# The first two slots of a seven-product MLP in plain form, x parts made in place, no splits on GpSimd

## The chip, the cores and the metric

One core of a Trainium2 chip runs the whole program. The metric is the device time in microseconds (us) of one execution, as the median of several. The engines are TensorE (PE, with its weight loads as PEld), VectorE (DVE), ScalarE (ACT), GpSimd (POOL) and SyncE (SP), which here only issues DMAs; GpSimd issues DMAs too.

## The reference

Linear attention, then two MLPs, all in float32:

```
kv  = einsum("bhsd,bhse->bhde", k, v)            # 4 batches, 8 heads, 576 tokens, 64 wide
o   = einsum("bhsd,bhde->bhse", q, kv)
x   = o / sqrt(mean(o*o) + 1e-6) * g_norm        # as 2304 tokens x 512
y   = softplus(x @ w1) @ w2                      # 512 -> 2048 -> 512
out = leaky_relu(y @ w3, 0.01) @ w4              # 512 -> 2048 -> 512
```

## The kernel before, in words

**Attention** runs over 16 units (a batch and a pair of heads). T transposes q and k and forms k^T v, O multiplies, `normal` normalizes, and X (four units behind) transposes the result into the tile `xy`, which holds x^T for all tokens. Units up to 9 use the PSUM banks 0 to 3, later ones 0 and 1, with further banks for O and X.

**Split numbers.** A float32 operand of an MLP is kept as a high part, rounded by a ScalarE copy (`fp32r`), and a low part, what is left, by a VectorE or GpSimd subtraction (`split_part`, lines 711 and 706; `split_pair`, 655 and 659; `split_w2`, 612 and 618). A product is three matmuls: high by high, high by low, low by high. The weights come as 64-bit floats and are decoded into float32 first (`decode_w`: one ScalarE and three VectorE operations, lines 578 to 596, with two raw buffers).

**Seven products.** The first layer of an MLP works on blocks of 2 x 2: two halves of the 512 inputs, two token halves of 384, two feature blocks of 128. A slot `s` multiplies one pair of token halves (`t = s // 2`, 768 tokens; three pairs, NTP = 3) by 256 features (`u = s % 2`). It uses the form with seven block products instead of eight, of six matmuls each (`product`, line 802). For this, sums of blocks of x are made by `x_part`: parts 0, 3 and 5 are plain blocks, and parts 1, 2, 4 and 6 are differences made one from the other through two tiles `xt` (line 740), and each is split. The sums of the weights' blocks come from `split_pair` (line 638). `after` puts the seven results together: copies (line 825) and additions (line 832) into `cA` and `cB`, the activation (839 or 845), and the split of the result (853, 858). `quarter` is the second layer (lines 900 and 916, 48 matmuls in a slot from the third on), and adds into `xy`.

**Where the parts of x lie.** The tile `xe` (in `ra`) holds seven parts for the pair in work. For the first pair they are made in place during attention, and stored to a DRAM scratch `xscr`. For the next pairs, at first sight, `x_part` makes the difference parts during the even slot in two stages in `rc` and stores them to `xscr` (line 758); in the odd slot, when a product has used its old part, `x_load` loads the new one on GpSimd's queue (line 784), and splits the plain blocks from `xy` or from a load on SP's queue (line 775). The eight groups of 512 features (four for each MLP) go over the same three pairs, with x parts from `xscr` after the first group of an MLP.

**The order of the work** is not the program's. Every operation is handed to a planner (`Plan`) with a cost for each engine that may do it, what it reads and writes, and a due time worked back from the matmuls. The planner plays the run through, picks for every engine what is due first, and so fixes the order of each engine's queue and the engine for what several could do (`either`: VectorE or GpSimd). An engine's queue is in order. The planner holds a load issued on GpSimd's queue for done after 1.0 us, one on SP's queue after its transfer and fixed times.

```
wst, xe: ra;  raw weights, xt, cA[0], cB: mf;  stages: rc;  cA[1], second raw weight pair: lf
slot s:  seven times  product(s, i); after(s, i); [x_part or x_load for t + 1]; a seventh of the quarters
```

Of the kernel before, what the change touches and what calls it, by code (L numbers as in the profile page):

```python
# [19 lines left out]
class Plan:  # L20
# [8 lines left out]
    IDLE = 40.0  # L29
    DMA_ISSUE, DMA_START, DMA_DONE = 0.57, 1.1, 1.0  # L30

    def __init__(self):
# [30 lines left out]
    def span(self, o):  # L63
        if "S" in o["cost"]:
            return self.DMA_ISSUE + self.DMA_START + o["cost"]["S"] + self.DMA_DONE
        return min(o["cost"].values())

    def run(self):
        for o in reversed(self.ops):
            for s in o["succ"]:  # L70
                o["due"] = min(o["due"], s["due"] - self.LAT - self.span(o))
        free = {e: 0.0 for e in ("PE", "A", "D", "P", "S", "N")}
        dma = 0.0
# [15 lines left out]
        while True:  # L89
            best = None  # L90
            for e, c in cand.items():
                if not c:
                    continue
                t = max(free[e], min(o["at"][e] for o in c))
# [15 lines left out]
            o["eng"], o["start"] = e, t  # L110
            if e == "S":
                free[e] = t + self.DMA_ISSUE
# [16 lines left out]
def linear_attention_two_mlps(  # L129
# [32 lines left out]
    nc = tc.nc  # L162
# [57 lines left out]

    SIZE = {"ra": 70, "mf": 24, "rb": 54, "rc": 12, "lf": 7}
    bufs = {}
# [41 lines left out]
    sqr = const.tile([P, DM], I32, name="sqr")  # L264
    raw = [Reg("mf", at * KI, [DM, 2], I32) for at in (0, 4)]

    SRAW = (("mf", 8), ("lf", 0))
    sraw = [Reg(n, at * KI, [4, 256]) for n, at in SRAW]
# [63 lines left out]
    def copy_to(out, in_, n, reads, writes):  # L332
# [222 lines left out]
    def decode_w(F, which, a_reg):  # L555
        ph, f = F // NF, F % NF
        src = ((w1, w2), (w3, w4))[ph][which]
        ri = chunk_no[0] % 2
        chunk_no[0] += 1
        r_, t_ = raw[ri].ap, sqr  # L560
        low, high = r_[:, :, 0], r_[:, :, 1]

        def f_l(e):
            if which == 0:
                nc.sync.dma_start(
# [3 lines left out]
            else:  # L569
# [3 lines left out]

        rk, tk, ak = raw[ri].keys(), [("sqr",)], a_reg.keys()
        op({"S": 1.46}, f_l, (), rk)
        op(
            {"A": t_a(DM)},
            lambda e: nc.scalar.activation(  # L578
                a_reg.ap.bitcast(F32), high.bitcast(F32), AF.Copy, scale=2.0 ** -112
            ), rk, ak,  # L580
# [24 lines left out]

    def split_w2(F, i, beside=False):
        for m in range(2):
# [8 lines left out]
            op(  # L616
                either(DM, beside),
                lambda e, d_=d_, w_=w_: ENG[e].tensor_tensor(
# [13 lines left out]

    def split_pair(i, u, beside=False):
        r, w_ = sraw[i], wst[u]

        def combine(j, a, b, sign):
            def fn(e):
                ENG[e].tensor_tensor(r[:, j, :], r[:, a, :], r[:, b, :], sign)

            op(either(256, beside), fn, part(r, a) + part(r, b), part(r, j))  # L640

        def parts(j, at, n):
# [18 lines left out]
            op({"A": t_a(m)}, hi, sk, hk)  # L661
            op(either(m, beside), lo, sk + hk, lk)


        parts(1, 0, 3)
        combine(1, 0, 1, ALU.add)
# [33 lines left out]

    def split_part(e_, src, sk, beside=False):
        n = 2 * BN
# [16 lines left out]
    def x_part(tp, i, stages=()):  # L719


        def B(j, k_):
            return x_block(tp, j, k_)

        if i in PLAIN:
            src, sk = B(*PLAIN[i])
            if not stages:
                split_part(xe[i], src, sk, True)
            op(
                {"S": 1.2}, lambda e: nc.sync.dma_start(out=whole(tp, i), in_=src()),  # L730
                sk, [("xs", tp, i)],
            )
            return
# [4 lines left out]
        def minus(t, a, b):  # L738
            def fn(e):
                ENG[e].tensor_tensor(xt[t].ap, a[0](), b[0](), ALU.subtract)  # L740

            op(either(2 * BN, not stages), fn, a[1] + b[1], xt[t].keys())
            return T_(t)
# [8 lines left out]
        if stages:  # L752
            e_ = stages[stage_no[0] % len(stages)]
            stage_no[0] += 1
        split_part(e_, src, sk, not stages)
        op(
# [5 lines left out]
    def flat(e_):  # L762
        return Reg(e_.name, e_.at, [4 * BN])

    xt_no = [0]

    def x_load(tp, i, at_hand):
# [3 lines left out]
        if i in PLAIN:  # L771
# [16 lines left out]
    def u_bank(s, which):  # L788

        return (s % 2, 2, 3)[which] if s else (2, 3, 3)[which]  # L790

    def product(s, i):
# [19 lines left out]
        op({"PE": 6 * t_mm[BN]}, fn, wk + e_.keys(), [("ps", bank)])  # L812

    def after(s, i):

# [19 lines left out]

        def act(dst, src, n, reads, writes):
            if s < 2 * NG * NTP:
                op(
                    {"A": t_a(n)}, lambda e: nc.scalar.activation(dst(), src(), AF.Softplus),  # L839
                    reads + [("set", 0)], writes + [("set", 1)],  # L840
                )
                return
            op(
                {"A": t_a(n)},
                lambda e: nc.scalar.activation(dst(), src(), AF.Prelu, alpha=0.01),  # L845
                reads + [("set", 1)], writes,
            )

        def parts(c, g):
            n = 2 * BN  # L850
            gk = g.keys(0, 4 * n)
            op(
                {"A": t_a(n)}, lambda e: nc.scalar.activation(g[:, 0, :, :], c.ap, AF.Copy),  # L853
                c.keys(), gk,
            )
            op(
                {"D": t_d(n)},
                lambda e: nc.vector.tensor_tensor(  # L858
                    g[:, 1, :, :], c.ap, g[:, 0, :, :].bitcast(F32), ALU.subtract
                ),  # L860
                c.keys() + gk, g.keys(4 * n),
            )

        if i == 0:
# [7 lines left out]
        elif i == 4:  # L872
            plus(cB, 0, U, bu)
            act(lambda: cB.ap, lambda: cB.ap, 2 * BN, cB.keys(), cB.keys())
            parts(cB, gB[s % 2])
        elif i == 5:
            plus(cA_, 1, W, bw)
            act(lambda: cA_[:, 1, :], lambda: cA_[:, 1, :], BN, ck(cA_, 1), ck(cA_, 1))
        else:
            act(lambda: cA_[:, 0, :], lambda: U, BN, bu, ck(cA_, 0))  # L880
            parts(cA_, gA[s % 3])
# [66 lines left out]
    def norm_done(e):  # L948
# [3 lines left out]
        )  # L952
        buf(p, "rc", F32R)
        buf(p, "lf", F32)
# [16 lines left out]
    for i in range(NU + XL):  # L971
# [4 lines left out]
        if i >= XL:  # L976
# [17 lines left out]
       + [(t + "r", i) for t in "qkv" for i in range(2)])  # L994
    split_w2(0, 0, True)
    op({"N": 0.0}, norm_done, (), granules("rc", "lf") + [("sql", 0)]
# [3 lines left out]
    decode_pair(2, 1, 1)  # L1000
    split_w2(2, 1, True)

# [4 lines left out]
    for s in range(2 * NT2 + 2):  # L1007
# [74 lines left out]
```

## Time and profile before

| | us |
|---|---|
| median of 3 runs (lowest, highest) | 858.88 (854.82, 860.17) |
| the profiled execution | 858.63 |
| its span, first to last instruction | 856.9 |

Busy in the span: TensorE 830.3 us, its weight loads 772.8, VectorE 572.2, ScalarE 449.5, GpSimd 97.6. DMA moved 172.73 MB. In the rows below an arrow `out<-in` names tiles, `L802` a line of the kernel, and `[2.44 <-DMA ra<-xscr]` says that the engine sat idle 2.44 us before and what it waited for. An instruction's length in a row overlaps a little with the next one's of the same engine.

### The profile page before, as it was taken

To read this page: it belongs to the slowest core of one execution; us is meant where nothing else is said; L and a number is where in the kernel's file an instruction comes from. 1 tells how busy PE (TensorE), PEld (TensorE's weight loads), DVE (VectorE), ACT (ScalarE), POOL (GpSimd) and SP (SyncE) were. 2 spreads that over 40 slices of the span, in tenths; PEclk is the share of its full clock that TensorE was granted. 3 is DMA by queue.
4 is the path that set the end of the run, shared out by engine and by line. 5 is a ranking of instruction groups with operands and counts; after the bars stand their busy time and mean duration, and the time that the engine had idled before them with its cause. 6 is when DMAs were issued, how large, how long until landed. Compare 5 with 4: busy or idle time off the path is not lost.

```text
span 856.9 us, 11971 instructions
## 1 busy us (share of the span) xinstructions
PE 830.3 (97%) x4512; PEld 772.8 (90%) x4512; DVE 572.2 (67%) x911; ACT 449.5 (52%) x730; POOL 97.6 (11%) x152
## 2 busy tenths in 40 slices
PE   7998879999999999999999999999999999999997
PEld 5877769999999999999999998898988889898986
DVE  2779958786558673877778875766568855854332
ACT  1567847666445553645456665755455544553340
POOL 1476210000000000000000000000000000100000
PEclk9999999999999999999999999999999999999999
DMA  9984679667527646547757867645635852643613
GB/s 280 319 260 173 202 283 342 228 209 229 188 88 235 202 142 225 170 153 229 244 198 236 310 242 269 223 165 190 227 95 181 275 172 82 203 147 93 203 49 98
DMA packets 80024, 172.73 MB, mean 202 GB/s; under 512 B 11616, under 2 KB 54112, under 8 KB 79968
## 3 DMA queue, kind: packets, MB, share of 16 engines
q1 hardware_dynamic: 66720, 99.63, 35.0%
q0 software_dynamic: 13248, 72.36, 25.4%
q8 instruction: 35, 0.57, 0.3%
q14 instruction: 21, 0.17, 0.1%
HBM read 141.30 MB, written 30.67 MB: 201 GB/s over the span
## 4 chain that ended last, share of the span: by engine, by line
PE 88%; DMA 5%; DVE 4%; ACT 2%; issue 1%; POOL 0%; SPq 0%; POOLq 0%; DVEq 0%
PE ps L802 38%; PE ps L900 22%; PE ps L916 22%; PE ps L436 2%; DMA ra<-xscr 1%; DMA mf<-in_moe_w_in_dram 1%; PE ps L405 1%; DMA xscr<-rc 1%; PE ps L397 1%; PE ps L528 1%; DMA qa<-in_q_dram 1%; PE ps L442 1%; PE ps L408 1%; DVE xn L506 0%; DVE ra L659 0%
## 5 line engine op out<-in xcount | busy, mean ns | idle before, releaser
L802 PE MATMUL ps<-ra 128*128 128x384 f32 x2016 | 406.0, 336 | 10.0 <-DMA ra<-xscr 7.7
L802 PEld LDWEIGHTS ps<-ra 128*128 128x128 f32 x2016 | 357.4, 188 | 27.0 <-issue 6.5
L900 PE MATMUL ps<-rb 128*128 128x384 f32 x1152 | 227.1, 335 | 0.0
L916 PE MATMUL ps<-rb 128*128 128x512 f32 x864 | 225.0, 394 | 0.4 <-ACT xy L678 0.4
L900 PEld LDWEIGHTS ps<-rb 128*128 128x128 f32 x1152 | 202.6, 188 | 0.0
L916 PEld LDWEIGHTS ps<-rb 128*128 128x128 f32 x864 | 159.7, 188 | 24.7 <-ACT xy L678 1.1
L832 DVE TENSOR_TENSOR mf<-ps,mf 128x384 f32<-128x384 f32 x120 | 66.7, 557 | 156.5 <-PE ps L802 124.5
L784 POOL DMA_DIRECT2D ra<-xscr x92 | 49.2, 535 | 653.4 <-PE ps L802 605.5
L825 ACT ACTIVATE mf<-ps 128x384 f32<-128x384 f32 x120 | 58.7, 492 | 99.2 <-PE ps L802 98.5
L683 DVE TENSOR_TENSOR xy<-ps,xy 128x384 f32<-128x384 f32 (+1 forms) x126 | 77.4, 614 | 30.1 <-PE ps L916 20.8
L858 DVE TENSOR_TENSOR rb<-mf,rb 128x768 fp32r<-128x768 f32 x72 | 68.4, 951 | 1.9 <-ACT rb L853 1.8
L711 ACT ACTIVATE ra<-mf 128x768 fp32r<-128x768 f32 x58 | 48.7, 841 | 29.8 <-PE ps L802 28.6
L853 ACT ACTIVATE rb<-mf 128x768 fp32r<-128x768 f32 x72 | 61.0, 847 | 2.1
L706 DVE TENSOR_TENSOR ra<-mf,ra 128x768 fp32r<-128x768 f32 x55 | 53.5, 972 | 12.3 <-ACT ra L711 12.0
L845 ACT ACTIVATE mf<-mf 128x768 f32<-128x768 f32 (+1 forms) x36 | 26.6, 739 | 60.1 <-DVE mf L832 60.1
L839 ACT ACTIVATE mf<-mf 128x768 f32<-128x768 f32 (+1 forms) x36 | 26.5, 735 | 45.5 <-DVE mf L832 45.5
L590 DVE SCALAR_TENSOR_TENSOR sqr<-mf,sqr 128x512 int32<-128x512 int32 x64 | 46.9, 733 | 1.2
L578 ACT ACTIVATE mf<-mf 128x512 f32<-128x512 f32 x34 | 22.6, 666 | 27.4 <-DMA mf<-in_moe_w_in_dram 19.8
L678 ACT ACTIVATE xy<-ps 128x384 f32<-128x384 f32 (+1 forms) x33 | 17.4, 531 | 18.0 <-PE ps L900 14.7
L858 DVE TENSOR_TENSOR rb<-lf,rb 128x768 fp32r<-128x768 f32 x24 | 22.9, 954 | 3.7 <-ACT rb L853 3.7
L832 DVE TENSOR_TENSOR lf<-ps,lf 128x384 f32<-128x384 f32 x24 | 13.4, 558 | 16.9 <-PE ps L802 16.8
L596 DVE SCALAR_TENSOR_TENSOR mf<-mf,sqr 128x512 int32<-128x512 int32 x34 | 23.7, 698 | 0.4
(97 smaller groups left out, 646.5 us busy)
## 6 DMA issues: line engine op xcount, KB each, us to landing
ra<-xscr POOLq DMA_DIRECT2D x92, 768.0 KB, 6.0
mf<-xscr SPq DMA_DIRECT2D x54, 384.0 KB, 5.5
mf<-in_moe_w_in_dram SPq DMA_DIRECT2D x32, 512.0 KB, 4.4
mf<-in_moe_w_out_dram SPq DMA_DIRECT2D x32, 512.0 KB, 4.0
xscr<-rc SPq DMA_DIRECT2D x20, 768.0 KB, 4.0
xscr<-xy SPq DMA_DIRECT2D x18, 384.0 KB, 4.8
qa<-in_q_dram SPq DMA_DIRECT2D x16, 256.0 KB, 5.2
ka<-in_k_dram SPq DMA_DIRECT2D x16, 256.0 KB, 5.1
```

The lines of the kernel that those rows point to most:

```text
L590: lambda e: nc.vector.scalar_tensor_tensor(t_, low, 29, t_, ALU.logical_shift_right, ALU.bitwise_or), rk + tk, tk,
L683: {"D": t_d(n)}, lambda e: nc.vector.tensor_tensor(dst, src, dst, ALU.add),
L706: ENG[e].tensor_tensor(e_[:, 1, :, :], src(), e_[:, 0, :, :].bitcast(F32), ALU.subtract)
L711: {"A": t_a(n)}, lambda e: nc.scalar.activation(e_[:, 0, :, :], src(), AF.Copy),
L784: lambda e: nc.gpsimd.dma_start(out=flat(xe[i]).ap, in_=xscr[7 * tp + i]),
L802: nc.tensor.matmul(o, w_[:, a, c:c + P], e_[:, b, kk, :], start=(not on and kk == 0 and n == 0), stop=(kk == 1 and n == 2), skip_group_che ...
L825: {"A": t_a(BN)}, lambda e: nc.scalar.activation(c[:, m, :], src, AF.Copy),
L832: lambda e: nc.vector.tensor_tensor(c[:, m, :], src, c[:, m, :], ALU.add),
L853: {"A": t_a(n)}, lambda e: nc.scalar.activation(g[:, 0, :, :], c.ap, AF.Copy),
L858: lambda e: nc.vector.tensor_tensor(g[:, 1, :, :], c.ap, g[:, 0, :, :].bitcast(F32), ALU.subtract),
L900: nc.tensor.matmul(y[:, :BN], w_[m][:, a, js], G_[:, b, m, :], start=(u == 0 and m == 0 and i == 0), stop=(u == 1 and m == 1 and i == 2),)
L916: nc.tensor.matmul(y, G_[:, a, m, js], w_[m][:, b, :], start=(u == 0 and m == 0 and i == 0), stop=(u == 1 and m == 1 and i == 2),)
```

## The change

- Slots 0 and 1 (t = 0) use a plain form with eight block products (`plain`). They read four split blocks of x, not sums, and write banks 2 and 3 only. `first_blocks` splits these four and stores them unsplit. One more block of W is split for each slot (`wx`, in the place of part 3 of x).
- For t = 1 and 2 `x_part` makes the parts in place in `xe`, in the odd slot before. The parts of the first pair are made in slot 5 from blocks loaded back in slot 4 (`blocks_back`, into `rc`) and stored for later groups. The second MLP's first group is staged as before.
- `either` goes: all splits, sums and differences are VectorE's. GpSimd keeps copies of q and k, some small operations of `normal`, and its DMA loads.
- The planner counts a load on GpSimd's queue (`"G"`) with issue, start, transfer and end, as one on SP's queue.
- `lf` grows to 8 KB and `mf` shrinks to 23: `cA[1]` moves to `mf` and the second raw buffer to `lf`, which exists only after attention; the first six weight chunks use one raw buffer.

```diff
-        if "S" in o["cost"]:
-            return self.DMA_ISSUE + self.DMA_START + o["cost"]["S"] + self.DMA_DONE
+        if self.DMA_BY.keys() & o["cost"].keys():
+            return self.DMA_ISSUE + self.DMA_START + sum(o["cost"].values()) + self.DMA_DONE
...
-    raw = [Reg("mf", at * KI, [DM, 2], I32) for at in (0, 4)]
+    raw = [Reg(n, at * KI, [DM, 2], I32) for n, at in (("mf", 0), ("lf", 4))]
...
+    wx = [Reg("ra", at * KI, [2, 256]) for at in (18, 20)]
...
-        ri = chunk_no[0] % 2
+        ri = chunk_no[0] % 2 if chunk_no[0] >= 6 else 0
...
-        op(either(n, beside), lo, sk + hk, lk)
+        op({"D": t_d(n)}, lo, sk + hk, lk)
...
-            {"P": 1.0},
+            {"G": 2.25},
             lambda e: nc.gpsimd.dma_start(out=flat(xe[i]).ap, in_=xscr[7 * tp + i]),
...
-        return (s % 2, 2, 3)[which] if s else (2, 3, 3)[which]
+        return (s % 2, 2, 3)[which]
...
+    FIRST = {(0, 0): 0, (1, 0): 1, (0, 1): 5, (1, 1): 6}
+
+    def first_blocks():
+        for (j, k_), at in FIRST.items():
+            src, sk = x_block(0, j, k_)
+            split_part(xe[at], src, sk)
+            x_store(0, {(0, 0): 0, (1, 1): 3, (1, 0): 5, (0, 1): 7 * NTP}[j, k_], src, sk)
...
+    def plain(s, k_):
+        c, g_ = (cB, gB[s % 2]) if k_ else (cA[s % 2], gA[s % 3])
+        w_ = wst[s % 2]
+        for m in range(2):
+            o = ps[2 + m][:, :BN]
+            for j in range(2):
+
+                e_, W_, part_ = xe[FIRST[j, k_]], *((wx[s], 0) if m + j == 0 else (w_, 2 * m + j - 1))
...
+                op({"PE": 6 * t_mm[BN]}, fn, wk + e_.keys(), [("ps", 2 + m)])
+            from_psum(c[:, m, :], o, BN, 2 + m, c.keys(4 * BN * m, 4 * BN * (m + 1)))
+        act(s, lambda: c.ap, lambda: c.ap, 2 * BN, c.keys(), c.keys())
+        parts(c, g_)
...
             if i - XL == 2 * NPAIR - 1:
-                for part_ in range(7):
-                    x_part(0, part_)
+                first_blocks()
...
         for i in range(7):
+            if t == 0 and i in (0, 3):
+                plain(s, i // 3)
             if t < NT2:
-                product(s, i)
-                after(s, i)
-                if t + 1 < NT2 and u == 0 and t + 1 in fresh:
+                if t > 0:
+                    product(s, i)
+                    after(s, i)
+                if s == 2 * NTP - 2 and i == 0:
+                    blocks_back()
+
+
+                if t + 1 in fresh and t + 1 > NTP and u == 0:
                     x_part((t + 1) % NTP, i, xstage)
-                if t + 1 < NT2 and u == 1:
+                elif t + 1 < NTP and u == 1:
+                    x_part((t + 1) % NTP, i)
+                elif t + 1 == NTP and u == 1:
+                    x_part(0, i, B=back)
+                elif t + 1 < NT2 and u == 1:
                     x_load((t + 1) % NTP, i, t + 1 in fresh)
```

## Rows read from the trace of the kernel before

**Rows 1.** totals of the page: busy time, share of the span, instructions of each engine.

```profile
PE 830.3 (97%) x4512; PEld 772.8 (90%) x4512; DVE 572.2 (67%) x911; ACT 449.5 (52%) x730; POOL 97.6 (11%) x152
```

**Rows 2.** stretches: length, busy PE, PEld, DVE, ACT, POOL (instructions); PEclk, DMA share, GB/s.

```profile
40.00:94.00 54.00, 49.20 (x338) 40.48 (x336) 48.15 (x93) 39.11 (x82) 34.73 (x37) 1.00 0.66 224
94.00:110.00 16.00, 11.98 (x65) 11.02 (x64) 14.91 (x20) 14.70 (x23) 4.76 (x4) 0.98 0.65 221
110.00:120.00 10.00, 7.71 (x39) 7.23 (x38) 4.99 (x7) 2.63 (x5) 0.64 (x2) 0.86 1.05 391
120.00:160.00 40.00, 36.64 (x208) 35.74 (x207) 29.42 (x45) 24.96 (x44) 2.64 (x5) 1.00 0.76 271
160.00:174.00 14.00, 14.00 (x83) 14.00 (x82) 11.28 (x19) 10.31 (x18) 1.58 (x3) 1.00 0.69 220
174.00:200.00 26.00, 26.00 (x152) 26.00 (x151) 17.34 (x27) 15.11 (x26) 1.58 (x3) 1.00 0.57 194
```

**Rows 3.** TensorE's waits from 40 to 94 us: total us, times, longest.

```profile
PE ps L397 <- ACT qt L353: 2.6, 4, 0.8
PE ps L436 <- DVE xn L506: 1.1, 2, 0.9
```

**Rows 4.** TensorE's waits from 94 to 160 us.

```profile
PE ps L802 <- DMA ra<-xscr: 7.7, 4, 2.4
PE ps L802 <- ACT lf L825: 1.4, 1, 1.4
```

**Rows 5.** chain that ended last, 90 to 160 us: start, length, what.

```profile
106.29 9.87 DMA xscr<-rc
...
128.37 2.08 PE ps L802 x12
```

**Rows 6.** TensorE in order of time: start, length, line, count, idle before.

```profile
109.31 2.13 PE L802 MATMUL ps<-ra 128*128 128x384 f32 x6 [2.44 <-DMA ra<-xscr]
...
114.69 1.28 PE L802 MATMUL ps<-ra 128*128 128x384 f32 x6 [2.29 <-DMA ra<-xscr]
```

**Rows 7.** lines 706, 740, 638, 618, 659: length, VectorE busy, GpSimd busy, then as above.

```profile
30.00:124.00 94.00, 8.45 (x8) 12.36 (x6) 0.98 0.74 248
30.00:124.00 94.00, 4.42 (x4) 8.71 (x4) 0.98 0.74 248
30.00:124.00 94.00, 2.54 (x3) 3.67 (x5) 0.98 0.74 248
30.00:124.00 94.00, 0.69 (x1) 4.84 (x3) 0.98 0.74 248
30.00:124.00 94.00, 5.01 (x3) 1.81 (x1) 0.98 0.74 248
```

**Rows 8.** VectorE's groups from 180 to 400 us: busy us, mean ns of one.

```profile
L706 DVE TENSOR_TENSOR ra<-mf,ra 128x768 fp32r<-128x768 f32 x21 | 20.1, 956 | 5.7 <-ACT ra L711 5.7
...
L832 DVE TENSOR_TENSOR mf<-ps,mf 128x384 f32<-128x384 f32 x35 | 19.5, 558 | 48.9 <-PE ps L802 48.9
L590 DVE SCALAR_TENSOR_TENSOR sqr<-mf,sqr 128x512 int32<-128x512 int32 x20 | 13.8, 690 | 0.4
...
L618 DVE TENSOR_TENSOR rb<-lf,rb 128x512 fp32r<-128x512 f32 x6 | 4.1, 684 | 0.0
```

**Rows 9.** VectorE in order of time, 47 to 54 us.

```profile
47.72 0.41 DVE L638 TENSOR_TENSOR mf<-mf 128x256 f32<-128x256 f32 x1
...
53.51 1.21 DVE L659 TENSOR_TENSOR ra<-mf,ra 128x1024 fp32r<-128x1024 f32 x1
```

**Rows 10.** GpSimd and VectorE in order of time, 75 to 77 us.

```profile
75.50 2.43 POOL L740 TENSOR_TENSOR mf<-xy,mf 128x768 f32<-128x768 f32 x1
...
76.16 2.85 DVE L659 TENSOR_TENSOR ra<-mf,ra 128x1024 fp32r<-128x1024 f32 x1
```

**Rows 11.** VectorE's groups from 60 to 100 us.

```profile
L590 DVE SCALAR_TENSOR_TENSOR sqr<-mf,sqr 128x512 int32<-128x512 int32 x3 | 3.7, 1219 | 0.0
...
L638 DVE TENSOR_TENSOR mf<-mf 128x256 f32<-128x256 f32 x2 | 2.1, 1065 | 0.0
```

More of the change, by code (lines that the diff above doesn't have):

```diff
@@ L30 @@
     DMA_ISSUE, DMA_START, DMA_DONE = 0.57, 1.1, 1.0
+    DMA_BY = {"S": "S", "G": "P"}
     def __init__(self):
@@ L71, in run @@
                 o["due"] = min(o["due"], s["due"] - self.LAT - self.span(o))
-        free = {e: 0.0 for e in ("PE", "A", "D", "P", "S", "N")}
+        free = {e: 0.0 for e in ("PE", "A", "D", "P", "S", "G", "N")}
         dma = 0.0
@@ L93, in run @@
                     continue
-                t = max(free[e], min(o["at"][e] for o in c))
+                t = max(free[self.DMA_BY.get(e, e)], min(o["at"][e] for o in c))
                 o = min(
@@ L110, in run @@
             o["eng"], o["start"] = e, t
-            if e == "S":
-                free[e] = t + self.DMA_ISSUE
+            if e in self.DMA_BY:
+                free[self.DMA_BY[e]] = t + self.DMA_ISSUE
                 dma = max(dma, t + self.DMA_ISSUE + self.DMA_START) + o["cost"][e]
@@ L616, in split_w2 @@
             op(
-                either(DM, beside),
+                {"D": t_d(DM)},
                 lambda e, d_=d_, w_=w_: ENG[e].tensor_tensor(
@@ L631, in part, with split_pair @@
         return r.keys(1024 * j, 1024 * (j + n))
-    def split_pair(i, u, beside=False):
+    def split_pair(i, u, first=False):
         r, w_ = sraw[i], wst[u]
@@ L638, in fn @@
                 ENG[e].tensor_tensor(r[:, j, :], r[:, a, :], r[:, b, :], sign)
-            op(either(256, beside), fn, part(r, a) + part(r, b), part(r, j))
+            op({"D": t_d(256)}, fn, part(r, a) + part(r, b), part(r, j))
         def parts(j, at, n):
@@ L661, in parts @@
             op({"A": t_a(m)}, hi, sk, hk)
-            op(either(m, beside), lo, sk + hk, lk)
+            op({"D": t_d(m)}, lo, sk + hk, lk)
+        if first:
+            x_, hk = wx[u], wx[u].keys()
+            op({"A": t_a(256)}, lambda e: nc.scalar.activation(x_[:, 0, :], r[:, 0, :], AF.Copy),
+               part(r, 0), hk)
+            op(
+                {"D": t_d(256)},
+                lambda e: nc.vector.tensor_tensor(
+                    x_[:, 1, :], r[:, 0, :], x_[:, 0, :].bitcast(F32), ALU.subtract
+                ), part(r, 0) + hk, hk,
+            )
         parts(1, 0, 3)
@@ L713, in split_part, with x_store, x_part @@
         )
-        op(either(n, beside), lo, sk + hk, lk)
+        op({"D": t_d(n)}, lo, sk + hk, lk)
     def whole(tp, i):
         return xscr[7 * tp + i][:, :2 * BN].rearrange("p (a n) -> p a n", a=2)
-    def x_part(tp, i, stages=()):
-        def B(j, k_):
-            return x_block(tp, j, k_)
+    def x_store(tp, i, src, sk):
+        op(
+            {"S": 1.2}, lambda e: nc.sync.dma_start(out=whole(tp, i), in_=src()),
+            sk, [("xs", tp, i)],
+        )
+    def x_part(tp, i, stages=(), B=None):
+        stored = B is not None
+        B = B or (lambda j, k_: x_block(tp, j, k_))
         if i in PLAIN:
@@ L727, in x_part @@
             if not stages:
[L728 to L732, printed above, removed]
+                split_part(xe[i], src, sk)
+            if not stored:
+                x_store(tp, i, src, sk)
             return
@@ L740, in fn @@
                 ENG[e].tensor_tensor(xt[t].ap, a[0](), b[0](), ALU.subtract)
-            op(either(2 * BN, not stages), fn, a[1] + b[1], xt[t].keys())
+            op({"D": t_d(2 * BN)}, fn, a[1] + b[1], xt[t].keys())
             return T_(t)
@@ L754, in x_part @@
             stage_no[0] += 1
-        split_part(e_, src, sk, not stages)
+        split_part(e_, src, sk)
         op(
@@ L812, in product, with act @@
         op({"PE": 6 * t_mm[BN]}, fn, wk + e_.keys(), [("ps", bank)])
+    def act(s, dst, src, n, reads, writes):
+        if s < 2 * NG * NTP:
+            op(
+                {"A": t_a(n)}, lambda e: nc.scalar.activation(dst(), src(), AF.Softplus),
+                reads + [("set", 0)], writes + [("set", 1)],
+            )
+            return
+        op(
+            {"A": t_a(n)},
+            lambda e: nc.scalar.activation(dst(), src(), AF.Prelu, alpha=0.01),
+            reads + [("set", 1)], writes,
+        )
@@ new lines, in parts @@
+    def parts(c, g):
+        n = 2 * BN
+        gk = g.keys(0, 4 * n)
+        op(
+            {"A": t_a(n)}, lambda e: nc.scalar.activation(g[:, 0, :, :], c.ap, AF.Copy),
+            c.keys(), gk,
+        )
+        op(
+            {"D": t_d(n)},
+            lambda e: nc.vector.tensor_tensor(
+                g[:, 1, :, :], c.ap, g[:, 0, :, :].bitcast(F32), ALU.subtract
+            ),
+            c.keys() + gk, g.keys(4 * n),
+        )
+    FIRST = {(0, 0): 0, (1, 0): 1, (0, 1): 5, (1, 1): 6}
@@ new lines, in first_blocks, with back, blocks_back @@
+    def first_blocks():
[3 more added lines that the diff above has]
+            x_store(0, {(0, 0): 0, (1, 1): 3, (1, 0): 5, (0, 1): 7 * NTP}[j, k_], src, sk)
+    def back(j, k_):
+        x_ = xb[j, k_]
+        return (lambda: x_.ap), x_.keys()
+    def blocks_back():
+        for (j, k_), x_ in xb.items():
+            i = {(0, 0): 0, (1, 1): 3, (1, 0): 5, (0, 1): 7 * NTP}[j, k_]
+            op(
+                {"S": 1.2}, lambda e, x_=x_, i=i: nc.sync.dma_start(out=x_.ap, in_=whole(0, i)),
+                [("xs", 0, i)], x_.keys(),
+            )
@@ new lines, in plain, with fn @@
+    def plain(s, k_):
[5 more added lines that the diff above has]
+                e_, W_, part_ = xe[FIRST[j, k_]], *((wx[s], 0) if m + j == 0 else (w_, 2 * m + j - 1))
+                def fn(e, j=j, o=o, e_=e_, W_=W_, part_=part_):
+                    for kk in range(2):
+                        at = part_ * 256 + kk * P
+                        for n, (a, b) in enumerate(((0, 0), (0, 1), (1, 0))):
+                            nc.tensor.matmul(
+                                o, W_[:, a, at:at + P], e_[:, b, kk, :],
+                                start=(j == 0 and kk == 0 and n == 0),
+                                stop=(j == 1 and kk == 1 and n == 2),
+                            )
+                wk = W_.keys() if W_ is wx[s] else [
+                    k for a in range(2)
+                    for k in w_.keys(7168 * a + 1024 * part_, 7168 * a + 1024 * (part_ + 1))
+                ]
+                op({"PE": 6 * t_mm[BN]}, fn, wk + e_.keys(), [("ps", 2 + m)])
+            from_psum(c[:, m, :], o, BN, 2 + m, c.keys(4 * BN * m, 4 * BN * (m + 1)))
+        act(s, lambda: c.ap, lambda: c.ap, 2 * BN, c.keys(), c.keys())
+        parts(c, g_)
@@ L834, in plus @@
             )
[L836 to L862, printed above, removed]
         if i == 0:
@@ L952, in norm_done @@
         )
-        buf(p, "rc", F32R)
+        buf(p, "rc", F32)
         buf(p, "lf", F32)
@@ L1000, in linear_attention_two_mlps @@
     decode_pair(2, 1, 1)
-    split_w2(2, 1, True)
+    split_w2(2, 1)
     NT2 = 2 * NG * NTP
```

41 lines of the change are left out of this document (20 added, 21 removed).

## The prediction

> **What bounds the kernel now.** I read the totals first: TensorE is busy for 97% of the span and no other engine is near it [rows 1], so a gain has to come out of the few stretches in which TensorE waits, and every added matmul has to be paid. The table of stretches says where these are [rows 2]: 4.8 us of 54.0 idle between 40 and 94 us (the end of attention), 4.0 of 16 from 94 to 110, 2.3 of 10 from 110 to 120, 3.4 of 40 from 120 to 160, nothing from 160 to 200. After 160 us TensorE simply works through its matmuls; only the start can be shortened. Then the list of waits, for the two halves of the start: up to 94 us TensorE waits for ScalarE's copies of q^T (2.6 us) and for VectorE's normalized x [rows 3]; after 94 us 7.7 us stand at four waits for the load of x parts from the DRAM scratch, and 1.4 us at a copy of ScalarE behind the change of its function table [rows 4]. The chain tells why the loads are late: a staged part waits 9.9 us for its store to DRAM, and its load comes on top [rows 5]. The chip's clock also fell: the granted clock is 0.86 in the stretch with the gaps, and six products that take 1.28 us took 2.13 [rows 2, 6].
>
> **The change, part by part.** The sum is made against the profiled execution's own 858.63 us (span 856.9, 1.7 around it); the median of the runs, 858.88, is 0.25 above it, which I neglect.
>
> *No staging of x for t = 1, 2, 3.* Twelve 768 KB loads on GpSimd's queue go (four per t; 92 become 80), with their store-to-load round trips. The four waits went to these loads: **-7.7 us** [rows 4]. Bounds: 0, if TensorE then waits for the same part out of VectorE, to -7.7. I take all of it and put the new wait into a term of its own. The clock's dip goes with the gaps: 2.13 - 1.28 = **-0.9** [rows 6] (bounds 0 and -1.5; the dip covers more than the one group).
>
> *Plain form in slots 0 and 1.* 48 matmuls in place of 42, twice: 12 more. Twelve take 2.08 us in the dense stretch [rows 5]: **+2.1**, not hidden, for TensorE is the bound.
>
> *Earlier work for the gaps of attention.* Slot 0 needed differences of x made one behind the other on GpSimd; now it needs four split blocks. Slot 1 had to wait for bank 1, which attention uses to the end; plain slots use banks 2 and 3 alone, free once attention's unit 9 is through. Up to 72 matmuls (slot 0 and half of slot 1: three output buffers) can stand in the gaps up to 94 us, where 42 stood. That changes no sum of work, only fills the 4.8 us [rows 2]: bounds 0 and -4.8. The waits there are short ones behind ScalarE and VectorE [rows 3], and queues are in order, so not all are filled: three quarters, **-3.6**. The wait of 1.4 us behind the table load [rows 4] loses its place: in slot 1 TensorE writes its last two banks without the output buffer being free, and slot 2 begins in bank 0. Bounds 0 and -1.4; I take **-1.4**.
>
> *GpSimd's splits go to VectorE.* Between 30 and 124 us GpSimd did 19 of these operations: 6 splits of x, 4 differences, 5 combinations of W, 3 splits of W2, 1 of W [rows 7]. VectorE gets: four splits of first blocks where it had one of that pair, +3 x 0.956; combinations +5 x 0.41; W2 +3 x 0.684; W +0.96; two new splits of 256 columns +2 x 0.41. That is 8.9 us [rows 8, 9]. It loses: six additions from PSUM (three in each of the two slots) at 0.558, 3.3 us [rows 8]; in their place come eight copies out of PSUM where ScalarE had six, on either engine (bounds 0 and 4.5; half, 2.2). And it loses the time in which GpSimd held it up. At 75.50 us a difference runs on GpSimd for 2.43 us; a split that starts on VectorE at 76.16 takes 2.85 instead of 1.21 [rows 9, 10]: it ends where GpSimd's end and its own time lead. From 60 to 100 us three decode steps were 0.53 longer than later ones, two combinations 0.66 each, this split 1.64: 4.5 us [rows 8 to 11]. Net +8.9 - 3.3 + 2.2 - 4.5 = +3.3 us for VectorE, against 5.9 us of its own idle time up to 94 us and 1.1 to 110 [rows 2]. Hidden, so **0**; if the cover is gone (nothing of the 4.5 comes back, all copies on VectorE) it is +10.1, 3.1 more than the 7.0 free.
>
> *Parts made in place.* A part of the next pair may be written only when TensorE has used the old one in the odd slot, and must be there when the even slot reaches its product. VectorE has 11 operations a pair for it (7 splits, 4 differences, 10.5 us at 0.956 [rows 8]). At t = 1 and 2 it had these before, at t = 3 only three splits: +8 x 0.956 = 7.6 us in slot 5, today 160 to 174 us, where VectorE has 14.0 - 11.3 = 2.7 free; 4.9 us are over, and the next stretch has 8.7 free [rows 2]. The parts are wanted one after the other over a whole slot, so most of it can slip without harm. The trace shows no such wait, so bounds: 0 and 10.5 for each of three changes of pair, had they no cover. Nearest row is slot 5 with 4.9: I take **+2.0** in all (0.5 at the first, 1.5 at the third).
>
> *Queues.* SP gets four loads of stored blocks (384 KB, slot 4) and one more block store, loses three plain loads, and the four sum-part stores of pair 0 move from attention to slot 5. They stand there behind VectorE's splits with weight loads for the next group behind them; those have a slot of cover. Costed at 0. The new accounting of GpSimd's loads only reorders issues; the loads of later pairs have a slot of time and cost TensorE nothing today [rows 2].
>
> Sum: -7.7 - 0.9 + 2.1 - 3.6 - 1.4 + 0 + 2.0 = -9.5: **849.1 us**.
>
> **The rivals.** *Same, about 857 us: VectorE takes over.* VectorE's table share up to 110 us is 63.1 of 70 [rows 2]. If what GpSimd held up does not come back, its work ends 3.1 us later than the room allows, the attention's gaps stay and the table wait too: -7.7 - 0.9 + 2.1 + 2.0 + 3.1 = -1.4, or 857.2. For it: part of the waits up to 94 us hangs on VectorE's normalized x already [rows 3]. Against it: the 2.85 us row, whose excess belongs to a GpSimd operation that goes away [rows 10]. On this the Trainium skill (Perfetto Trace Analysis, Optimizing Scalar/DVE Operations) has a rule that speaks against the change: where VectorE is saturated, moving work to ScalarE or even GpSimd may make sense, though the two share a read port and it might not help. By the rule's first half the time would be this rival's, by its caveat the forecast's; the row of 2.85 us bears out the caveat.
>
> *Slower, about 863 us: parts behind the products.* VectorE's queue is in order. If in slots 1, 3 and 5 its splits stand behind operations that wait for TensorE's products, or those products' results behind the splits, TensorE stands still at each change of pair for up to 10.5 us. Without any such wait the sum is 847.1; it turns slower from 3.8 us per change on, and at half of the full price (5.25 each) gives 847.1 + 15.8 = 862.9. For it: slot 5's surplus of 4.9 us. Against: each slot from the second on has 48 matmuls of the other layer, four times 2.08 us [rows 5], that need no part of x.
>
> **How the numbers follow.** The forecast's case gets 0.64 (VectorE fits its room), VectorE's takeover 0.27, the parts' wait 0.09. About 1%, 8.6 us, is what a measurement here can tell from no change: the line is at 850.3. The forecast's own range is 845 (every gap filled, no new wait: 858.63 - 7.7 - 0.9 + 2.1 - 4.8 - 1.4 = 845.9, and the dip's upper bound) to 853 (half of the attention term, four us of new waits); 0.55 of its 0.64 lie under the line. Faster 0.55; same 0.09 + 0.27 + 0.02 = 0.38; slower 0.07, since a small wait at the changes still ends within 1%. The range runs from 844 to 858: it leaves out the slower case and the third of the takeover that lies above its sum.
>
> **What would show it.** Right: 4524 matmuls and 80 loads on GpSimd's queue; no wait for a scratch load and no dip of the clock up to 160 us; GpSimd without tensor-tensor splits, VectorE's decode steps near 0.69 and the W split near 1.21 in attention; TensorE's idle time from 40 to 94 near 1.2 us; dense matmuls from about 110 us, some 10 us earlier than today's 153. Wrong: waits of TensorE on the split of x at the three changes of pair over 3.8 us each, or attention ending later with VectorE full.

## The result, and the profile after

The changed kernel takes **845.23 us** (median of 4 runs, 843.24 to 847.33), the kernel before 857.19 beside it (4 runs, 854.82 to 860.17): the ratio is 0.9859, 95% interval 0.981 to 0.9908. That is faster, by 12 us, where 9.5 were forecast. The profiled execution took 843.24 us, 15.4 less than the one of before.

The totals of the page and the table of stretches (columns as in [rows 2]):

```profile
PE 824.9 (98%) x4524; PEld 772.0 (92%) x4524; DVE 572.9 (68%) x918; ACT 450.5 (54%) x730; POOL 68.7 (8%) x134
```

```profile
40.00:94.00 54.00, 49.85 (x339) 42.00 (x338) 43.01 (x89) 35.90 (x73) 14.84 (x30) 1.00 0.50 163
94.00:110.00 16.00, 16.00 (x94) 16.00 (x93) 14.83 (x21) 14.35 (x24) 0.00 (x0) 1.00 0.98 361
110.00:120.00 10.00, 10.00 (x60) 10.00 (x59) 8.29 (x13) 6.87 (x13) 0.00 (x0) 1.00 0.49 185
120.00:160.00 40.00, 40.00 (x233) 40.00 (x232) 33.58 (x51) 29.19 (x50) 0.00 (x0) 1.00 0.49 172
```

The 12 more matmuls are there (4524 against 4512, [rows 1]). From 94 us on TensorE is never idle. Before, it lost 4.0, 2.3 and 3.4 us in the second, third and fourth row, with a granted clock of 0.86 in the third [rows 2]. In the first row, the end of attention, it still loses 54.0 - 49.85 = 4.15 us, against 4.8.

The three longest of TensorE's six waits over the whole run (total us, times, longest):

```profile
PE ps L398 <- DVE qp L343: 6.1, 2, 4.0
PE ps L437 <- DVE xn L507: 2.6, 3, 1.3
PE ps L891 <- DVE ra L717: 1.1, 1, 1.1
```

No wait for a scratch load is left, and none after 94 us; before there were four, 7.7 us [rows 4]. TensorE in order of time shows where the dense part begins (start, length, idle before):

```profile
87.03 2.20 PE L891 MATMUL ps<-ra 128*128 128x384 f32 x11 [1.13 <-DVE ra L717]
...
92.62 5.47 PE L891 MATMUL ps<-ra 128*128 128x384 f32 x30
97.93 1.20 PE L816 MATMUL ps<-ra 128*128 128x384 f32 x6
```

From 92.62 us, where before it was 153, matmul follows on matmul to the end. VectorE's groups from 60 to 100 us, as in [rows 11]:

```profile
L591 DVE SCALAR_TENSOR_TENSOR sqr<-mf,sqr 128x512 int32<-128x512 int32 x4 | 2.7, 687 | 0.1
...
L639 DVE TENSOR_TENSOR mf<-mf 128x256 f32<-128x256 f32 x4 | 1.7, 413 | 0.0
...
L660 DVE TENSOR_TENSOR ra<-mf,ra 128x1024 fp32r<-128x1024 f32 x1 | 1.2, 1215 | 0.0
```

The decode step is back from 1219 ns to 687, the sum of W from 1065 to 413, the long split of W from 2.85 us [rows 10] to 1.215. And yet VectorE's busy time between 40 and 94 us fell only by 5.1 us (43.0 for 48.15), since it does GpSimd's work now.

**A part that is not the change's.** TensorE's first matmuls run at about half speed, and when that ends differs from profile to profile. In these two, eight matmuls of 128 columns, of before and then of after:

```profile
14.54 2.07 PE L436 MATMUL ps<-kvm,qt 128*128 128x128 f32 x8
...
18.08 2.07 PE L436 MATMUL ps<-kvm,qt 128*128 128x128 f32 x8
```

```profile
11.79 1.73 PE L406 MATMUL ps<-va,kp 128*128 128x128 f32 x8
...
13.87 1.16 PE L437 MATMUL ps<-kvm,qt 128*128 128x128 f32 x8
```

Before, they still take 2.07 us at 18 us; after, 1.16 from 13.9 us on. The ratio is near that of the clock's two levels, 1.2 and 2.4 GHz, though the granted clock reads 1.00 from 14 to 16 us in both, with 9 matmuls in one and 14 in the other, and over the whole start too (first before, then after):

```profile
14.00:16.00 2.00, 2.00 (x9) 1.77 (x10) 0.96 (x3) 0.00 (x0) 0.62 (x1) 1.00 1.14 350
...
0.00:94.00 94.00, 82.99 (x522) 66.87 (x522) 67.12 (x142) 52.91 (x109) 44.82 (x58) 1.00 0.81 255
```

```profile
14.00:16.00 2.00, 2.00 (x14) 1.47 (x14) 1.49 (x4) 0.60 (x1) 0.62 (x1) 1.00 1.09 382
...
0.00:94.00 94.00, 82.91 (x542) 68.10 (x543) 65.98 (x146) 52.67 (x108) 25.73 (x54) 1.00 0.71 221
```

TensorE is idle for nearly the same time up to 94 us (11.0 and 11.1 us), but 542 matmuls are done instead of 522: 20 more, at 0.173 us (twelve take 2.08 [rows 5]) 3.5 us. No kernel was profiled with both an early and a late rise, so that the runs of one kernel differ for this reason (843.24 and 843.28 against 847.18 and 847.33 here) is likely and not shown.

So the 15.4 us between the two profiles are: 3.5 from the start, 13.0 from 94 to 160 us (387 matmuls for 312, 75 x 0.173; 9.7 us of it idle time), 0.7 from two small waits later that are gone, less 2.1 for the 12 matmuls. Together 15.1. Of the 3.3 us that are not idle time some 1.4 are the dip of the clock: in the kernel before six matmuls of 384 columns take 2.13 us and the three behind them 1.16, where 1.20 and 0.68 are usual:

```profile
111.24 1.16 PE L900 MATMUL ps<-rb 128*128 128x384 f32 x3
...
118.94 1.20 PE L802 MATMUL ps<-ra 128*128 128x384 f32 x6
119.98 0.68 PE L900 MATMUL ps<-rb 128*128 128x384 f32 x3
```

The rest (the first matmuls behind a gap, counts at the edges) was not taken apart.

### The profile page after: what moved, and what is told of

Read it like the earlier page. It is cut to its first block, busy times and chain, and to the rows that moved or that the text cites. A ratio compares the mean times of both kernels' runs of the same rounds, so it can differ in the third digit from the quotient of the medians.

```text
span 841.5 us, 11960 instructions
## 1 busy us (share of the span) xinstructions
PE 824.9 (98%) x4524; PEld 772.0 (92%) x4524; DVE 572.9 (68%) x918; ACT 450.5 (54%) x730; POOL 68.7 (8%) x134
## 4 chain that ended last, share of the span: by engine, by line
PE 96%; DVE 1%; ACT 1%; DMA 1%; issue 0%; POOL 0%; SPq 0%; ACTq 0%
PE ps L816 40%; PE ps L964 24%; PE ps L980 24%; PE ps L406 2%; PE ps L891 2%; PE ps L437 2%; PE ps L398 1%; PE ps L529 1%; PE ps L409 1%; DMA qa<-in_q_dram 1%; PE ps L443 0%; PE ps L402 0%; ACT xy L517 0%; DVE xy L694 0%; DVE xn L507 0%
## 5 line engine op out<-in xcount | busy, mean ns | idle before, releaser
L816 PE MATMUL ps<-ra 128*128 128x384 f32 x1932 | 387.6, 335 | 0.0
L816 PEld LDWEIGHTS ps<-ra 128*128 128x128 f32 x1932 | 342.8, 188 | 14.0
L924 DVE TENSOR_TENSOR mf<-ps,mf 128x384 f32<-128x384 f32 x138 | 76.7, 556 | 169.7 <-PE ps L816 138.4
L917 ACT ACTIVATE mf<-ps 128x384 f32<-128x384 f32 x138 | 67.8, 492 | 111.5 <-PE ps L816 110.5
L850 DVE TENSOR_TENSOR rb<-mf,rb 128x768 fp32r<-128x768 f32 x96 | 91.2, 950 | 3.8 <-ACT rb L845 3.7
L845 ACT ACTIVATE rb<-mf 128x768 fp32r<-128x768 f32 x96 | 81.3, 847 | 2.6
L837 ACT ACTIVATE mf<-mf 128x768 f32<-128x768 f32 (+1 forms) x48 | 32.8, 683 | 61.4 <-DVE mf L924 61.4
L831 ACT ACTIVATE mf<-mf 128x768 f32<-128x768 f32 (+1 forms) x48 | 33.3, 693 | 46.4 <-DVE mf L924 46.3
L591 DVE SCALAR_TENSOR_TENSOR sqr<-mf,sqr 128x512 int32<-128x512 int32 x35 | 24.1, 689 | 0.8
L837 ACT ACTIVATE mf<-ps 128x384 f32<-128x384 f32 x24 | 11.7, 488 | 17.3 <-PE ps L816 17.2
L597 DVE SCALAR_TENSOR_TENSOR lf<-lf,sqr 128x512 int32<-128x512 int32 x30 | 20.6, 686 | 0.4
L656 ACT ACTIVATE ra<-mf 128x768 fp32r<-128x768 f32 (+1 forms) x18 | 17.1, 952 | 6.2 <-PE ps L816 3.6
```

Source lines behind the costliest of these rows:

```text
L597: lambda e: nc.vector.scalar_tensor_tensor(a_reg.ap, a_reg.ap, -(1 << 31), t_, ALU.bitwise_and, ALU.bitwise_or), tk + ak, ak,
L816: nc.tensor.matmul(o, w_[:, a, c:c + P], e_[:, b, kk, :], start=(not on and kk == 0 and n == 0), stop=(kk == 1 and n == 2), skip_group_che ...
L850: lambda e: nc.vector.tensor_tensor(g[:, 1, :, :], c.ap, g[:, 0, :, :].bitcast(F32), ALU.subtract),
L917: {"A": t_a(BN)}, lambda e: nc.scalar.activation(c[:, m, :], src, AF.Copy),
L924: lambda e: nc.vector.tensor_tensor(c[:, m, :], src, c[:, m, :], ALU.add),
```

## The experiments

Theory A: the gain is the DRAM round trip of the staged parts, and the splits' move was neutral. Rival B: it is the time that GpSimd held VectorE up. Rival C: it is the planner's better knowledge of loads. The first three undo one part each of the changed kernel (845.2 us); the next four do parts alone on the kernel before (856.17 beside them).

**1. Splits open to GpSimd again.**

```diff
-            op({"D": t_d(m)}, lo, sk + hk, lk)
+            op(either(m, first), lo, sk + hk, lk)
...
-            split_part(xe[at], src, sk)
+            split_part(xe[at], src, sk, True)
...
-    split_w2(2, 1)
+    split_w2(2, 1, True)
```

> The changed kernel with the first splits and sums of x, W and W2 open to GpSimd again (the planner then gives it 4 splits of x, 3 of W, 8 sums and 4 splits of W2). Theory A, the gain is the DRAM round trip of the staged parts, and GpSimd's part in the splits was neutral: within 2 us of the changed kernel (843 to 849 us), no wait of TensorE after 94 us. Rival B, the gain is the time that GpSimd held VectorE up: 5 to 8 us above the changed kernel (850 to 853), with VectorE's long instructions back and TensorE waiting between 60 and 110 us.

848.68 us (847.38 to 850.17, ratio 0.9902, 0.9876 to 0.9927): 3.5 above the changed kernel, between the two theories' numbers, but with the waits that A ruled out. The table of stretches, then GpSimd, VectorE and TensorE in order of time:

```profile
40.00:94.00 54.00, 52.04 (x349) 44.51 (x348) 42.74 (x87) 33.48 (x69) 23.90 (x31) 1.00 0.46 150
94.00:110.00 16.00, 13.14 (x72) 11.63 (x71) 14.67 (x18) 13.00 (x23) 4.73 (x3) 1.00 0.88 323
110.00:120.00 10.00, 8.83 (x42) 8.36 (x43) 8.77 (x12) 5.57 (x11) 1.29 (x1) 0.83 0.56 226
```

```profile
97.26 1.73 POOL L622 TENSOR_TENSOR rb<-mf,rb 128x512 fp32r<-128x512 f32 x1 [13.81 <-ACT rb L616]
...
107.96 1.27 POOL L622 TENSOR_TENSOR rb<-lf,rb 128x512 fp32r<-128x512 f32 x1 [6.99 <-ACT rb L616]
```

```profile
97.76 2.05 DVE L853 TENSOR_TENSOR rb<-mf,rb 128x768 fp32r<-128x768 f32 x1
99.74 2.05 DVE L720 TENSOR_TENSOR ra<-mf,ra 128x768 fp32r<-128x768 f32 x1
...
108.06 1.72 DVE L600 SCALAR_TENSOR_TENSOR lf<-lf,sqr 128x512 int32<-128x512 int32 x1
109.70 0.95 DVE L853 TENSOR_TENSOR rb<-mf,rb 128x768 fp32r<-128x768 f32 x1
```

```profile
110.70 1.16 PE L967 MATMUL ps<-rb 128*128 128x384 f32 x5 [2.33 <-DVE rb L853]
```

Up to 94 us GpSimd's help is good: TensorE idles 2.0 us instead of 4.15. After 94 it is bad. GpSimd splits W2 at 97.26 for 1.73 us, until 98.99; VectorE's split, begun at 97.76, takes 2.05 instead of 0.95, which is the rest of GpSimd's time and 0.82 more; the next split, behind GpSimd's second one, is as long. At 108.06 a decode step takes 1.72 instead of 0.69. VectorE has no gap from 97.76 on, so these 3.2 us push back the split behind them, which TensorE waits for: it ends at 110.65, and TensorE stands still for 2.33 us until 110.70, with the clock at 0.83 in that stretch. The Trainium skill (SBUF — State Buffer, Who interferes with whom) says that a VectorE instruction with two SBUF inputs and a GpSimd instruction that reads SBUF exclude each other for their whole length, the second to issue waiting; these rows agree.

**2. Pairs 1 and 2 staged again.**

```diff
-                if t + 1 in fresh and t + 1 > NTP and u == 0:
+                if t + 1 in fresh and t + 1 != NTP and u == 0:
...
-                elif t + 1 < NTP and u == 1:
-                    x_part((t + 1) % NTP, i)
```

> The changed kernel with the parts of pairs 1 and 2 staged in rc, stored and loaded again as before; plain slots, pair 0 from stored blocks and the splits on VectorE stay. Theory A: waits for the scratch loads come back between 94 and 160 us, 6 to 10 us, and the kernel loses 7 to 12 us (852 to 857). Rival B: the loads were late because VectorE was, which is now free: 0 to 3 us lost (845 to 848).

850.59 us (848.36 to 851.29, ratio 0.9919, 0.9894 to 0.9944): 5.4 lost, less than A's 7 to 12, more than B's 3. TensorE's longest wait from 94 to 160 us:

```profile
PE ps L816 <- DMA ra<-xscr: 2.2, 2, 1.5
```

The round trip costs something even with VectorE rid of GpSimd, but 2.2 us of waits, not 7.7. This does not speak for B alone: the kernel keeps the new accounting, which by itself brings the waits down to 2.5 us (experiment 4), and the two were not separated here.

**3. The old accounting.**

```diff
-            {"G": 2.25},
+            {"P": 1.0},
```

> The changed kernel with the planner's old accounting of loads on GpSimd's queue (1.0 us). Theory A: no load of that queue is left before 180 us, so within 1 us of the changed kernel (844 to 847). Rival C, the gain is the planner's better knowledge of these loads: 3 us or more lost (848 to 853), with waits for scratch loads.

844.38 us (843.89 to 845.27, ratio 0.9852, 0.9831 to 0.9874): the same. With the parts in place the changed kernel issues its first load on GpSimd's queue at 181.09 us, and TensorE waits for none.

**4. The new accounting alone, on the kernel before** (the reverse of that edit, with the planner's lines).

> The kernel before with nothing changed but the planner's accounting of loads on GpSimd's queue (issue, start, transfer, end). Theory A, the round trip itself is too long for its slot: 855 to 859 us, waits for scratch loads stay at 5 us or more. Rival C, the order was wrong only because the planner held a load for done after 1 us: 848 to 853, the waits gone or under 3 us.

849.88 us (847.34 to 853.0, ratio 0.992, 0.9897 to 0.9944). Rival C is right here: nothing but the order of the queues is changed, and 6 to 7 us are gone. TensorE's waits from 94 to 160 us:

```profile
PE ps L803 <- DMA ra<-xscr: 2.5, 2, 2.3
PE ps L901 <- POOL rb L619: 1.0, 1, 1.0
```

7.7 us of waits for the scratch have become 2.5. The round trip is no shorter; the chain has these two (start, length):

```profile
101.42 10.19 DMA xscr<-rc
...
115.85 9.12 DMA ra<-xscr
```

Theory A took it for too long for its slot; with another order of the queues most of it fits. Which part of that order does it (earlier loads, or other matmuls ahead of the waiting products) was not followed.

**5. No splits on GpSimd, alone.**

```diff
-        return {"D": t_d(n), "P": t_p(n)} if beside else {"D": t_d(n)}
+        return {"D": t_d(n)}
```

> The kernel before with its splits, sums and differences kept off GpSimd, nothing else. Theory A, neutral alone, as VectorE gets more work (four differences and three splits more than in the changed kernel) and loses the time that it was held up: 856 to 861 us. Rival B: 850 to 855, VectorE's excess gone and the attention ending earlier. Undoing the same in the changed kernel cost about 3.5 us, which leaves room for either.

862.83 us, the median of seven: six lie between 861.04 and 864.04; one took 4355.88 us, for a reason that is not known, and the ratio leaves it out (1.0069, 1.0048 to 1.009). That is slower by about 6, more than A said and the opposite of B. TensorE's longest wait from 94 to 160 us, and two stretches:

```profile
PE ps L802 <- DMA ra<-xscr: 9.3, 3, 5.9
```

```profile
40.00:94.00 54.00, 46.91 (x307) 37.83 (x306) 46.14 (x87) 35.86 (x75) 17.93 (x34) 0.97 0.58 193
...
120.00:160.00 40.00, 36.45 (x197) 36.19 (x198) 26.43 (x41) 20.70 (x37) 2.58 (x5) 0.90 0.72 256
```

Seven splits and four differences of pair 0 stand on VectorE now, the staging begins later (the first store from `rc` at 100.88 us instead of 98.76), and the scratch wait grows from 7.7 to 9.3 us. That is not all of it: from 40 to 94 us TensorE idles 7.1 us instead of 4.8, and the granted clock is 0.90 from 120 to 160 us, where it was 1.00.

**6. Parts in place for pairs 1 and 2, alone.**

```diff
-                split_part(xe[i], src, sk, True)
+                split_part(xe[i], src, sk, tp == 0)
...
-            op(either(2 * BN, not stages), fn, a[1] + b[1], xt[t].keys())
+            op(either(2 * BN, tp == 0), fn, a[1] + b[1], xt[t].keys())
...
-                if t + 1 < NT2 and u == 0 and t + 1 in fresh:
+                if t + 1 < NT2 and u == 0 and t + 1 in fresh and t + 1 > NTP:
                     x_part((t + 1) % NTP, i, xstage)
-                if t + 1 < NT2 and u == 1:
+                if t + 1 < NTP and u == 1:
+                    x_part(t + 1, i)
+                elif t + 1 < NT2 and u == 1:
```

GpSimd may still split for pair 0; the parts of pairs 1 and 2 are VectorE's.

> The kernel before with the parts of pairs 1 and 2 made in place in the odd slot; seven products in slots 0 and 1, GpSimd's splits of pair 0 and the old accounting stay. Theory A: the waits for scratch loads are gone up to 160 us, 847 to 851 us, without the 2.1 us of the plain form. Rival, VectorE is late anyway: waits of TensorE on VectorE's splits take their place, 853 to 858.

847.24 us (842.75 to 848.2, ratio 0.9879, 0.984 to 0.9919). Stretches:

```profile
40.00:94.00 54.00, 48.61 (x326) 40.07 (x326) 48.86 (x90) 39.11 (x79) 34.43 (x33) 1.00 0.70 233
94.00:110.00 16.00, 16.00 (x94) 15.98 (x93) 15.62 (x20) 13.56 (x24) 3.12 (x2) 1.00 0.58 212
110.00:120.00 10.00, 10.00 (x60) 10.00 (x59) 9.87 (x17) 8.80 (x17) 0.00 (x0) 1.00 0.57 214
120.00:160.00 40.00, 40.00 (x233) 40.00 (x232) 33.18 (x51) 28.82 (x48) 2.02 (x3) 1.00 0.70 234
```

Dense from 94 us, as in the changed kernel, with VectorE at 9.9 of 10 in the third row: full, but in time.

**7. All but the plain form.**

```diff
-        return {"D": t_d(n), "P": t_p(n)} if beside else {"D": t_d(n)}
+        return {"D": t_d(n)}
...
-            {"P": 1.0},
+            {"G": 2.25},
```

(and the planner's lines and the edit of experiment 6.)

> The kernel before with parts in place for pairs 1 and 2, no splits on GpSimd and the new accounting: all of the change but the plain form (pair 0 is made in place by seven products' parts in attention, and loaded from the scratch for slot 6). Theory A, the plain form only costs its 12 matmuls: 841 to 845 us, 2 below the changed kernel. Rival E, the plain form is what lets TensorE run on at the end of attention, since sums of x would come late from VectorE: 848 to 854, with waits on VectorE between 60 and 100 us.

848.83 us (845.68 to 850.15, ratio 0.9896, 0.9855 to 0.9937): rival E's number. But the runs of experiments 1 to 7 differ by up to 6 us within one kernel, and the start's clock may be the reason; hence the last five.

**8. Matmuls ahead of the start**, in the changed kernel, where TensorE waits 4 us for q:

```diff
+        for _ in range(16):
+            nc.tensor.matmul(ps[7][:, :P], ident, ident, start=True, stop=True)
         plan.run()
```

> The changed kernel with 16 matmuls on the identity (128 by 128, into a bank not yet in use) ahead of everything on TensorE, where it waits 4 us for the first q. In the changed kernel's profile eight 128-column matmuls take 2.07 us until 12 us and 1.16 from 14 us on; in the kernel before they take 2.07 until 20 us. Theory D, the start runs at the lower clock until TensorE has been busy for a while, and the two levels of the runs (843 and 847) are early and late rises: the short form is reached by 9 us and the time falls 2 to 4 us below the changed kernel's runs, with less spread. Rival: the rise does not depend on earlier work: no change, or 0.5 us lost to the extra matmuls.

841.77 us (841.28 to 843.55, ratio 0.9828, 0.9801 to 0.9854), 3.5 below the changed kernel's 845.23, as theory D said. The two were not run side by side; by their ratios to the kernel before the gain is 0.3%, some 2.7 us, and the intervals overlap. Then the same lines in four kernels, run together:

> The kernel before with the 16 matmuls on the identity ahead of TensorE's work, so that all four kernels of this group start at the same clock. Theory D, the start's clock has nothing to do with the change: 2 to 5 us below the kernel before (852 to 855), with its waits for scratch loads of 6 to 9 us after 94 us unchanged. Rival: the earlier start only lengthens those waits, 856 to 858.

> The kernel before with parts of pairs 1 and 2 in place, and the 16 matmuls at the start. Theory F, making the parts in place is nearly the whole gain: 841 to 844 us, within 2 us of the changed kernel with the same start. Rival, plain form, VectorE's splits and accounting bring 3 us or more on top: 845 to 848.

> All of the change but the plain form, and the 16 matmuls at the start. Theory F: without GpSimd the seven parts of pair 0 hang on VectorE, TensorE waits for them before 110 us, 844 to 847 us, 3 to 5 above the changed kernel with the same start; the plain form is what pays for GpSimd's leaving. Rival: the plain form only costs its 12 matmuls, 839 to 841.

> The changed kernel with the 16 matmuls at the start, once more in the same group. All theories: 841 to 843 us. It is the measure for the other three: theory F wants the one with parts in place within 2 us of it and the one without the plain form 3 to 5 us above it.

| with the 16 matmuls | median us (lowest to highest) | ratio to before, 95% interval |
|---|---|---|
| the kernel before | 854.92 (853.46 to 857.21) | 0.9961 (0.9945 to 0.9978) |
| parts in place alone | 841.43 (840.05 to 841.66) | 0.9792 (0.9766 to 0.9819) |
| all but the plain form | 844.69 (844.61 to 847.66) | 0.9845 (0.9819 to 0.987) |
| the changed kernel | 841.78 (841.7 to 843.53) | 0.9805 (0.9778 to 0.9832) |

TensorE's start in the last of them (the row counts 32 for the 16):

```profile
1.37 6.12 PE L1124 MATMUL ps<-ident 128*128 128x128 f32 x32 [1.37 <-POOL ident masks.py:199]
...
9.05 1.16 PE L406 MATMUL ps<-va,kp 128*128 128x128 f32 x8
```

The short form, 1.16 us, is there at 9.05 us. The Trainium skill (TensorE: Matmul & The Clock Gate, What's actually happening) says that the array starts throttled and that activity releases it; the rows agree. The kernel before gains 3.8 us by it (858.72 to 854.92) with its waits for scratch loads at 7.5 us, which is theory D and not its rival.

The group settles the parts. Making the parts in place is worth 13.5 us and the whole change 13.1: theory F. Stretch 94 to 160 us of the kernel before and of parts in place, both with the 16 matmuls:

```profile
94.00:160.00 66.00, 57.92 (x321) 56.14 (x320) 49.20 (x72) 41.44 (x73) 6.37 (x9) 0.97 0.78 279
```

```profile
94.00:160.00 66.00, 66.00 (x383) 65.97 (x382) 58.69 (x85) 51.16 (x86) 5.40 (x6) 1.00 0.66 228
```

Taking GpSimd's splits away, with the accounting, costs 3.3; the plain form brings 2.9 back. Stretch 40 to 94 us of parts in place, all but plain, and changed:

```profile
40.00:94.00 54.00, 48.51 (x326) 40.13 (x327) 48.89 (x89) 39.30 (x78) 32.73 (x32) 1.00 0.72 240
```

```profile
40.00:94.00 54.00, 46.72 (x303) 37.76 (x303) 46.63 (x88) 35.63 (x74) 18.32 (x32) 0.97 0.60 195
```

```profile
40.00:94.00 54.00, 50.09 (x338) 42.55 (x339) 43.75 (x90) 35.32 (x72) 13.49 (x26) 1.00 0.55 174
```

TensorE idles 5.5, 7.3 and 3.9 us, and the granted clock of the second is 0.97. Without GpSimd the split parts of pair 0 come late from VectorE; TensorE in order of time in the kernel without the plain form:

```profile
84.23 2.18 PE L803 MATMUL ps<-ra 128*128 128x384 f32 x11 [1.81 <-DVE ra L707]
87.56 0.63 PE L529 MATMUL ps<-ident,xn 128*128 128x128 f32 x4 [1.15 <-DVE xn L507]
```

With the plain form TensorE idles 3.4 us less in this stretch, at the full clock, and that pays for its 12 matmuls; its own wait for a split there is still 1.1 us. One reservation: the starts are not alike in every run. In the profile of all but plain (846.49 us, 1.8 above its median) the long form comes back behind two waits of 0.54 and 0.64 us, and there the granted clock shows it, 0.79 from 8 to 16 us:

```profile
10.82 1.67 PE L406 MATMUL ps<-va,kp 128*128 128x128 f32 x8
```

```profile
8.00:16.00 8.00, 6.82 (x35) 5.49 (x35) 2.33 (x7) 1.03 (x2) 1.24 (x2) 0.79 1.10 331
```

The two fastest kernels, 841.43 and 841.78, are not told apart: parts in place alone do what the whole change does. Not run: parts in place, GpSimd's splits up to 94 us only and the plain form together, which experiment 1's first stretch suggests.

## Why the prediction was right or wrong

- *Staging, -7.7:* right for the waits. All four are gone, and experiment 6 shows it alone. But the length of the round trip is only part of the cause: with the planner's idea of a load's length put right (experiment 4) 2.5 of the 7.7 us are left. And the step is worth more than its waits: with equal starts it brings 13.5 us alone, 10.7 of them in the 62 more matmuls that are done from 94 to 160 us (at 0.173), where 8.1 us were idle.
- *Clock's dip, -0.9:* the direction right, too small. The two rows of it make 1.4 us, inside its bounds.
- *Plain form, +2.1:* the matmuls cost what was said; that the form pays for itself while VectorE makes all splits was not seen (experiment 1 has it beside GpSimd's splits, at 848.68 us; parts in place alone took 847.24). In the changed kernel the form is worth 2.9 us net.
- *Attention's gaps, -3.6:* wrong. 4.8 us became 4.15. I took fillers as free; in an in-order queue a filler is one more thing to wait for (1.13 us at 87.03 for the fourth block's split), and the waits for normalized x stayed (1.8 us from 40 to 94 us, 1.1 before [rows 3]). The waits for copies of q^T, 2.6 us before, are gone; what took them away was not looked into.
- *Table load, -1.4:* the wait is gone, but not for the reason given: in experiment 6, with seven products in both slots, only 0.4 us of it is left.
- *GpSimd's splits to VectorE, 0:* the five additions make 8.75 us, not 8.9, which changes nothing. The 4.5 us that GpSimd held VectorE up came back, row for row. But the zero hid two effects: losing GpSimd's help costs up to 94 us, and W2's splits on GpSimd cost after it (experiment 1, 3.5 us). Alone the step costs 6 us (experiment 5), near the takeover rival's mechanism, VectorE too late, which the plain form kept away. The rule of the Trainium skill on moving work to GpSimd (Perfetto Trace Analysis, Optimizing Scalar/DVE Operations) holds both ways in experiment 1: its first half up to 94 us (2.0 us idle instead of 4.15), its caveat after (the wait of 2.33 us).
- *In place, +2.0:* no wait at all at any of the three changes of pair. Slot 5 was worked out to be 4.9 us over VectorE's room; where those parts are made VectorE is busy for 17.05 of 20 us:

```profile
150.00:170.00 20.00, 20.00 (x117) 20.00 (x116) 17.05 (x25) 15.89 (x27) 0.00 (x0) 1.00 0.36 138
```

In experiment 6 it was full, 9.87 of 10 us, and still not late.

- *Not in the sum:* when TensorE reaches full speed, 3.5 us between the two profiles. The sum was made against a profile with a late rise.
- *The sign "dense from about 110 us, some 10 earlier than 153"* does not agree with itself; it was 92.62.

So -9.5 against 12 measured, and 13.1 where both kernels have the 16 matmuls. The mechanism was right, that the waits for staged parts are the gain; that the number lies so near is in part luck. The term of the gaps was 3 us too good, and the in-place term, 2 us too bad, the dip and the rest of what the staging cost made up for more than that. Plain form, gaps, table load and splits stood in the sum with 2.1 - 3.6 - 1.4 + 0 = -2.9; with the accounting they brought nothing measurable (13.1 with them, 13.5 without).

## What to carry to other kernels

Before replacing a staging path, tell the planner how long its transfers really take: that alone was worth 6 of the 12 us here. Try the parts of a change one by one: here one of them alone does as much as the whole. Judge a helper engine by stretch, not by kernel: the same GpSimd splits helped TensorE up to 94 us and stopped it after. While TensorE waits for its first data it can be given throw-away matmuls.

## What the runs showed of the hardware

Sixteen matmuls on the identity in TensorE's first, idle microseconds brought 3.8 us in the kernel before (858.72 to 854.92) and some 3 in the changed one. The granted clock in the profile's stretches does not show the slow start: it reads 1.00 while eight matmuls take 2.07 us instead of 1.16. It does show a later fall, 0.79 from 8 to 16 us in one profile.
